# PV moved into the middle of the score bursts of a sigmoid-attention + ReGLU kernel, with wider loads, a split first load and a held weight load

## The chip, the cores and the metric

The kernel runs on one core of one Trainium2 chip. The metric is the device time of one execution in microseconds. Before the change it is 450.13 us, the median of three runs (450.03 to 451.05). The profiled execution, from which all other numbers of this part come, has a span of 453.1 us.

## What is computed

Eight batches of sigmoid attention (12 heads, 448 tokens, head size 64) feed a gated feed-forward layer. Inputs and output are float32 in DRAM; the kernel computes in float16 with float32 sums.

```python
def _attn_ref(q, k, v):                      # (8, 12, 448, 64) each
    S = q.shape[2]
    scale = 1.0 / np.sqrt(q.shape[-1])
    scores = scale * np.matmul(q, k.transpose(0, 1, 3, 2)) - np.log(S)
    attn = 1.0 / (1.0 + np.exp(-scores))
    return np.matmul(attn, v).astype(np.float32)

def _moe_ref(x, w_gate, w_val, w_out):       # x: 3584 x 768, w_gate/w_val: 768 x 1536, w_out: 1536 x 768
    gate = np.maximum(x @ w_gate, 0.0)
    val = x @ w_val
    return (gate * val @ w_out).astype(np.float32)
# x is the attention output with the heads of a token side by side
```

## The kernel before

A batch has three head groups g of four heads, and each group seven chunks c of 64 keys. One `qk_unit` makes the scores of one chunk and four heads with four 64x64 matmuls that run side by side in the array, into two PSUM banks; ScalarE then takes the sigmoid of each bank into a PT tile. `pv` sums a group's seven PT tiles times v with 28 matmuls into two banks, which VectorE scales into the xT tiles. The feed-forward part is cut into pieces that are mixed in between: `gv` (letter f in a mix) makes one slice of gate and value in two banks; `down` (letter y) makes 128 rows of output in two banks.

```python
    PTp = ctx.enter_context(tc.tile_pool(name="PTp", bufs=12))
    # (cut) PSUM: two rings of four banks, taken in turn four by four, eight banks in all
    def next_ring():
        i = turn[0] // 4 % len(rings)
        turn[0] += 1
        return rings[i]

    def rows_of(src, b, r):
        return src[b].rearrange("(g r h) (t c) d -> r t g h (c d)", r=2, h=2, c=NCH)[r]

    def load(b, g0, g1, which="kqv", c0=0):
        for nm, t16, src in zip("kqv", tiles_of(b), (k, q, v)):
            if nm in which:
                for g in range(g0, g1):
                    for r in range(2):
                        nc.gpsimd.dma_start(
                            t16[64 * r : 64 * r + 64, g, :, c0 * D :],
                            rows_of(src, b, r)[:, g, :, c0 * D :],
                        )
    # (cut) the first keys and queries come as float32 over the queues of SyncE and ScalarE:
    # k head 0, k head 1, then q chunks 0 to 2; each in two halves of 64 partitions

    def qk_unit(b, g, c):
        ps = [bank("qk_ps") for _ in range(2)]
        for r in range(2):
            for hh in range(2):
                qk(qkT_tiles[(b, g)], r, hh, c, 0, NCH, ps[hh][64 * r : 64 * r + 64, 0:S])
        PT = PTp.tile([P, 2, 512], FP16, tag="PT", name="PT")
        for hh in range(2):
            sigmoid(PT[:, hh, 0:S], ps[hh][:, 0:S])          # ScalarE
        PT_tiles[(b, g, c)] = PT

    def pv(b, g, q0, qn, pieces):
        ps = [bank("pv_ps") for _ in range(2)]
        # (cut) 28 matmuls of 64x64
        for r in range(2):
            put_xT(b, 2 * g + r, q0, qn, ps[r][:, 0:qn])     # VectorE

    def dma_transposes(b, g):
        # (cut) two VectorE copies into rel, then
        nc.sync.dma_start_transpose(qkT_of(b, g)[:], rel[:].rearrange("p c x -> p (c x)"))

    for b in range(1, B):
        cuts = (0, 4, 7, 11, 16, 21) if b <= 2 else (0, 4, 8, 12, 16, 21)
        pv_at = {0: -1, 3: 0, 4: 1} if b <= 2 else {0: -1, 2: 0, 4: 1}
        # (cut) mixes of b == 1 and b == 2
        elif b % 2:
            mix = ["fyf", "fyf", "ffff", "fyf", "fyf"]
        else:
            mix = ["fff", "fyf", "fyf", "fff", "fyf"]
        for m in range(5):
            if m in pv_at and (b, m) != (1, 0):
                if m == 0:
                    pv_finish(b - 1)          # last group of the batch before, then its gv pieces queue up
                else:
                    pv_group(b, pv_at[m])
            for g, c in order[cuts[m] : cuts[m + 1]]:
                qk_unit(b, g, c)
            if b == 1:
                if m == 0:
                    load(2, 0, 1, "kq")
                    load_o()                  # the down weights wo, float32 4.7 MB in DRAM
                    load(2, 1, 2, "kq")
                    load(2, 2, 3, "kq")
                    load(2, 0, 3, "v")
                if m == 3:
                    dma_transposes(2, 0)
            # (cut) the others of b == 2: dma_transposes(2, 1) at m 0, (2, 2) at m 1
            ffn_mix(mix[m], hooks.get(m, ()))
```

So each batch has five bursts of 64x64 matmuls (m = 0 to 4), with gv and down pieces after each.

Of the kernel before, what the change touches and what calls it, by code (L numbers as in the profile page):

```python
# [10 lines left out]
FP32 = mybir.dt.float32  # L11
# [6 lines left out]
def kernel(  # L18
# [10 lines left out]
    nc = tc.nc  # L29

    B, H, S, D = q.shape
    DM, DF = moe_w_gate.shape
    NPAIR = H // 2
    NG = H // 4
    P = 128
    NCH = S // 64
# [3 lines left out]
    QCUT = 3  # L40
# [15 lines left out]
    ysbp = ctx.enter_context(tc.tile_pool(name="ysbp", bufs=4))  # L56
# [29 lines left out]
            )  # L86
        return in_tiles[b]

    def rows_of(src, b, r):
        return src[b].rearrange("(g r h) (t c) d -> r t g h (c d)", r=2, h=2, c=NCH)[r]  # L90

    def load(b, g0, g1, which="kqv", c0=0):
        for nm, t16, src in zip("kqv", tiles_of(b), (k, q, v)):
            if nm in which:
                for g in range(g0, g1):
                    for r in range(2):
                        nc.gpsimd.dma_start(  # L97
                            t16[64 * r : 64 * r + 64, g, :, c0 * D :],
                            rows_of(src, b, r)[:, g, :, c0 * D :],
                        )  # L100


    first32 = []
    k32 = [ysbp.tile([P, DM], FP32, tag="ysb", name="ysb") for _ in range(2)]
    q32 = ysbp.tile([P, DM], FP32, tag="ysb", name="ysb")
    q32v = q32[:, 0 : 2 * QCUT * D].rearrange("p (h x) -> p h x", h=2)
    for h in range(2):
        for r, eng in ((0, nc.sync), (1, nc.scalar)):
            rs = slice(64 * r, 64 * r + 64)
            eng.dma_start(k32[h][rs, 0 : NCH * D], rows_of(k, 0, r)[:, 0, h, :])  # L110
    for r, eng in ((0, nc.sync), (1, nc.scalar)):
        rs = slice(64 * r, 64 * r + 64)
        eng.dma_start(q32v[rs], rows_of(q, 0, r)[:, 0, :, 0 : QCUT * D])
    load(0, 1, 2, "kq")
    ident = const.tile([P, P], FP16, name="ident")
    make_identity(nc, ident[:])
    load(0, 2, 3, "kq")

    gate = const.tile([P, 2], FP16, name="gate")
# [26 lines left out]
    def load_o():  # L146
        for m0, m1 in ((0, 512), (512, DM)):
            nc.gpsimd.dma_start(
                wo[:, :, m0:m1], moe_w_out[:, m0:m1].rearrange("(c p) m -> p c m", p=P)
            )  # L150

    qkT_tiles = {}
# [3 lines left out]
    def keep_warm(count):  # L156
        ps = bank("warm_ps")
        for _ in range(count):
            nc.tensor.matmul(ps[:, 0:S], zeros[:, 0:P], zeros[:], start=True, stop=True)  # L159
# [6 lines left out]
    def put_xT(b, pr, q0, qn, src):  # L166
        nc.vector.tensor_scalar(  # L167
            out=xT_of(b, pr)[:, q0 : q0 + qn],
            in0=src,
            scalar1=XSCALE,  # L170
            scalar2=None,
            op0=AOP.mult,
        )
# [10 lines left out]
    def pe_transposes(b, g, ti, c0=0, c1=NCH):  # L184
        t16 = in_tiles[b][ti]
        qkT = qkT_of(b, g)
        trt = bank16("trt")
        for c in range(c0, c1):
            for h in range(2):
                nc.tensor.transpose(  # L190
                    trt[64 * h : 64 * h + 64, c * P : (c + 1) * P],
                    t16[:, g, h, c * D : (c + 1) * D],
                    ident[:],
                )
        nc.vector.tensor_copy(  # L195
            qkT[:, ti * NCH + c0 : ti * NCH + c1, :].rearrange("p c x -> p (c x)"),
            trt[:, c0 * P : c1 * P],
        )

    def dma_transposes(b, g):  # L200
        k16, q16, _ = in_tiles[b]
        rel = relp.tile([P, TW, P], FP16, tag="rel", name="rel")
        for ti, t16 in enumerate((k16, q16)):
            nc.vector.tensor_copy(  # L204
                rel[:, ti * NCH : (ti + 1) * NCH, :].rearrange("p c (h d) -> p h c d", h=2),
                t16[:, g].rearrange("p h (c d) -> p h c d", c=NCH),
            )
        nc.sync.dma_start_transpose(
            qkT_of(b, g)[:], rel[:].rearrange("p c x -> p (c x)")
        )  # L210
# [14 lines left out]
    def pv(b, g, q0, qn, pieces):  # L225
        v16 = in_tiles[b][2]
        ps = [bank("pv_ps") for _ in range(2)]
        for c in range(NCH):
            for hh in range(2):
                for r in range(2):  # L230
                    rows = slice(64 * r, 64 * r + 64)
                    nc.tensor.matmul(  # L232
                        ps[r][64 * hh : 64 * hh + 64, 0:qn],
                        v16[rows, g, hh, c * D : (c + 1) * D],
                        pieces[c][rows, hh, :],
                        start=(c == 0),
                        stop=(c == NCH - 1),
                        tile_position=(64 * r, 64 * hh),
                        skip_group_check=True,
                    )  # L240
        for r in range(2):
            put_xT(b, 2 * g + r, q0, qn, ps[r][:, 0:qn])


    class FirstSlot:
# [28 lines left out]
# [7 lines that stand above are left out]
            sigmoid(PT[:, hh, 0:S], ps[hh][:, 0:S])  # L281
        PT_tiles[(b, g, c)] = PT

    def pv_group(b, g):
        pv(b, g, 0, S, [PT_tiles.pop((b, g, c))[:, :, 0:S] for c in range(NCH)])
# [81 lines left out]
    def ffn_mix(kinds, hooks=()):  # L367
# [8 lines left out]
    nc.scalar.activation(gate[:], zeros[:, 0:2], AF.Sigmoid, bias=sig_bias, scale=qk_scale)  # L376
    keep_warm(10)
    k16, q16, _ = in_tiles[0]
    nc.vector.tensor_copy(k16[:, 0, 0, :], k32[0][:, 0 : NCH * D])
    nc.scalar.copy(k16[:, 0, 1, :], k32[1][:, 0 : NCH * D])  # L380
    nc.vector.tensor_copy(q16[:, 0, :, 0 : QCUT * D], q32v)
    pe_transposes(0, 0, 0, 0, 4)
    pe_transposes(0, 0, 1, 0, QCUT)
    pe_transposes(0, 0, 0, 4, NCH)
    slots = [FirstSlot(g, half) for half in range(2) for g in range(NG)]
    push_first(0, range(0, 4), False)

    after = {
        (0, 0): lambda: keep_warm(2),
        (0, 1): lambda: pe_transposes(0, 1, 0),  # L390
        (0, 2): lambda: pe_transposes(0, 1, 1),
        (1, 1): lambda: pe_transposes(0, 2, 0),
# [24 lines left out]
    order = [(g, c) for g in range(NG) for c in range(NCH)]  # L417

    def pv_finish(b):
        pv_group(b, NG - 1)  # L420
        push_gv(b, 0, S, range(NFC))
        if b % 2:
            push_down(b // 2, range(7))
# [2 lines left out]
    rings.insert(0, ctx.enter_context(tc.tile_pool(name="ring1", bufs=4, space=bass.MemoryType.PSUM)))  # L426
    turn[0] = 0

    def both(b, g):
        pe_transposes(b, g, 0)  # L430
        pe_transposes(b, g, 1)

    ffn_mix("ff", [(1, lambda: both(1, 0))])
    for b in range(1, B):
        cuts = (0, 4, 7, 11, 16, 21) if b <= 2 else (0, 4, 8, 12, 16, 21)
        pv_at = {0: -1, 3: 0, 4: 1} if b <= 2 else {0: -1, 2: 0, 4: 1}
        hooks = {}
        if b == 1:
            mix = ["f" * n for n in (4, 4, 3, 4, 3)]
            hooks = {1: [(1, lambda: both(1, 1))], 2: [(1, lambda: both(1, 2))]}  # L440
        elif b == 2:
            mix = ["fff", "fff", "ffy", "fyf", "fyf"]
        elif b % 2:
            mix = ["fyf", "fyf", "ffff", "fyf", "fyf"]
        else:
            mix = ["fff", "fyf", "fyf", "fff", "fyf"]
        for m in range(5):
            if m in pv_at and (b, m) != (1, 0):
                if m == 0:
                    pv_finish(b - 1)  # L450
                else:
                    pv_group(b, pv_at[m])
            for g, c in order[cuts[m] : cuts[m + 1]]:
                qk_unit(b, g, c)
            if b == 1:
                if m == 0:
                    load(2, 0, 1, "kq")
                    load_o()
                    load(2, 1, 2, "kq")
                    load(2, 2, 3, "kq")  # L460
                    load(2, 0, 3, "v")
                if m == 3:
                    dma_transposes(2, 0)
            elif b == 2:
                if m < 2:
                    dma_transposes(2, m + 1)
                if m == 1:
                    nc.gpsimd.tensor_copy(gate[0:1, :], qkT_tiles[(2, 2)][0:1, 0, 0:2])
                    load(3, 0, 3)
            elif m == 0:  # L470
                dma_transposes(b, 2)
                if b + 1 < B:
                    load(b + 1, 0, 3)
            if m >= 3 and b >= 2 and b + 1 < B:
                dma_transposes(b + 1, m - 3)
            ffn_mix(mix[m], hooks.get(m, ()))
    pv_finish(B - 1)
    for work in (gv_queue, y_queue):
# [32 lines left out]
```

## Time and profile before

| engine | busy us | share of the span |
|---|---|---|
| TensorE matmul (PE) | 434.1 | 96% |
| ScalarE (ACT) | 211.9 | 47% |
| VectorE (DVE) | 129.6 | 29% |
| GpSimd (POOL) | 97.7 | 22% |

In the page's second part the span is cut into 40 slices of 11.3 us. A digit is a busy share in tenths; PEclk is the TensorE clock that the throttle granted, DMA the busy share of the 16 DMA engines.

```profile
PE   5999997999999999999999999999999999999995
PEclk8599998999999999999999999999999999999999
DMA  9999999999989033982449323641333101100144
```

TensorE is busy throughout, but for the first slice and the seventh, at about 70 us. Its clock is low in the second slice. The DMA engines are full for the first 11 slices. Matmul records overlap, as a record of 350 ns is followed by the next after 189 ns, so that a busy share of 96% does not say how many matmuls of full pace fit: for that the distances between starts are read.

### The profile page before, as it was taken

What the parts mean: (1) busy time and instruction counts of PE and PEld (TensorE: products, weight loads), DVE (VectorE), ACT (ScalarE), POOL (GpSimd) and SP (SyncE); (2) the same over time, 40 slices, a digit from 0 to 9 for tenths busy, and PEclk for the clock granted to TensorE, in tenths of its full rate; (3) what the DMA queues carried; (4) which work ended last, traced back from release to release, by engine and by line L of the source; (5) the groups of instructions that cost most, each with busy time, mean ns of one, the idle gap of its engine ahead of it and who ended that gap; (6) DMA issues with size and microseconds to landing.
All of it is one profiled execution on the core that took longest, in us unless ns stands there. A gap on an engine that the chain in (4) does not pass through costs nothing.

```text
span 453.1 us, 8742 instructions
## 1 busy us (share of the span) xinstructions
PE 434.1 (96%) x3660; PEld 241.8 (53%) x3660; DVE 129.6 (29%) x247; ACT 211.9 (47%) x453; POOL 97.7 (22%) x163
## 2 busy tenths in 40 slices
PE   5999997999999999999999999999999999999995
PEld 2677864455555555455455554555455545555563
DVE  1343342222331322322331232312322222222211
ACT  2685666445544445545644445444545454222110
POOL 8755613086053000630026000300000000000000
PEclk8599998999999999999999999999999999999999
DMA  9999999999989033982449323641333101100144
GB/s 162 165 198 198 165 175 159 114 135 174 141 121 194 23 76 64 133 140 51 66 73 196 62 42 77 90 63 31 68 77 77 35 1 36 35 1 0 36 104 104
DMA packets 71078, 43.75 MB, mean 97 GB/s; under 512 B 36352, under 2 KB 67456, under 8 KB 71040
## 3 DMA queue, kind: packets, MB, share of 16 engines
q0 software_dynamic: 32960, 23.28, 36.8%
q1 hardware_dynamic: 37696, 19.54, 23.6%
q8 instruction: 28, 0.46, 0.4%
q10 hardware_dynamic: 384, 0.39, 0.3%
q14 instruction: 10, 0.08, 0.1%
HBM read 47.19 MB, written 11.01 MB: 128 GB/s over the span
## 4 chain that ended last, share of the span: by engine, by line
PE 87%; DMA 5%; DVE 3%; ACT 3%; issue 1%; ACTq 0%
PE g_ps L293 24%; PE v_ps L293 23%; PE ya L331 16%; PE yb L331 8%; PE qk_ps L215 7%; PE pv_ps L232 7%; DMA qkT<-rel 3%; DVE xT L167 3%; ACT PT L176 3%; PE trt L190 2%; DMA ysb<-in_q_dram 1%; DVE qkT L195 0%; ACTq L110 0%; PE warm_ps L159 0%; ACT ysb L345 0%
## 5 line engine op out<-in xcount | busy, mean ns | idle before, releaser
L176 ACT ACTIVATE PT<-qk_ps 128x448 f16<-128x448 f32 (+3 forms) x318 | 150.8, 596 | 65.2 <-PE qk_ps L215 65.1
L293 PE MATMUL g_ps<-xT,wg 128*128 128x448 f16 (+2 forms) x648 | 128.5, 334 | 0.8 <-DVE xT L167 0.2
L293 PE MATMUL v_ps<-xT,wv 128*128 128x448 f16 (+2 forms) x648 | 127.6, 333 | 0.0
L311 DVE TENSOR_TENSOR hT<-gate_sb,v_ps 128x448 f16<-128x448 f32 (+2 forms) x108 | 60.9, 569 | 229.0 <-PE v_ps L293 118.5
L331 PEld LDWEIGHTS <-hT 128*128 128x128 f16 x672 | 65.7, 98 | 47.1
L302 ACT ACTIVATE gate_sb<-g_ps 128x448 f32<-128x448 f32 (+2 forms) x104 | 55.3, 549 | 73.1 <-PE g_ps L293 71.3
L293 PEld LDWEIGHTS <-wv 128*128 128x128 f16 x648 | 62.7, 98 | 48.3 <-issue 2.0
L293 PEld LDWEIGHTS <-wg 128*128 128x128 f16 x648 | 59.9, 98 | 48.4 <-issue 9.7
L331 PE MATMUL ya<-wo,hT 128*128 128x512 f16 x336 | 77.1, 379 | 0.0
L215 PE MATMUL qk_ps<-qkT 64*64 64x448 f16 (+2 forms) x756 | 56.2, 347 | 9.1 <-DVE xT L167 4.8
L97 POOL DMA_DIRECT2D v<-in_v_dram x48 | 29.0, 620 | 140.6 <-PE qk_ps L215 135.5
L345 ACT ACTIVATE ysb<-yb 128x256 f32<-128x256 f32 x28 | 10.7, 383 | 93.2 <-PE yb L331 93.2
L215 PEld LDWEIGHTS <-qkT 64*64 64x64 f16 x756 | 25.3, 110 | 38.2 <-issue 25.9
L331 PE MATMUL yb<-wo,hT 128*128 128x256 f16 x336 | 41.3, 273 | 0.0
L232 PE MATMUL pv_ps<-PT,v 64*64 64x448 f16 (+2 forms) x756 | 38.1, 338 | 0.1
L167 DVE TENSOR_SCALAR xT<-pv_ps 128x448 f16<-128x448 f32 (+2 forms) x54 | 28.4, 568 | 23.2 <-PE pv_ps L232 23.2
L97 POOL DMA_DIRECT2D q<-in_q_dram x48 | 28.8, 622 | 18.7 <-DMA wo<-in_moe_w_out_dram 15.8
L339 DVE TENSOR_SCALAR ysb<-ya 128x512 f32<-128x512 f32 x28 | 19.4, 692 | 46.9 <-PE ya L331 46.9
L97 POOL DMA_DIRECT2D k<-in_k_dram x46 | 27.9, 640 | 14.3 <-DMA v<-in_v_dram 7.9
L232 PEld LDWEIGHTS <-v 64*64 64x64 f16 x756 | 20.5, 111 | 15.1 <-issue 7.3
L195 DVE COPY qkT<-trt 128x896 f16<-128x896 f16 (+2 forms) x14 | 7.5, 555 | 6.5 <-PE trt L190 6.4
L204 DVE COPY rel<-k 128x896 f16<-128x896 f16 x18 | 6.9, 385 | 1.6 <-DMA k<-in_k_dram 1.6
(24 smaller groups left out, 48.0 us busy)
## 6 DMA issues: line engine op xcount, KB each, us to landing
out_dram<-ysb SPq DMA_DIRECT2D x54, 192.0 KB, 2.7
v<-in_v_dram POOLq DMA_DIRECT2D x48, 112.0 KB, 5.2
k<-in_k_dram POOLq DMA_DIRECT2D x46, 112.0 KB, 6.4
q<-in_q_dram POOLq DMA_DIRECT2D x46, 112.0 KB, 5.1
wg<-in_moe_w_gate_dram POOLq DMA_DIRECT2D x6, 384.0 KB, 9.8
wv<-in_moe_w_val_dram POOLq DMA_DIRECT2D x6, 384.0 KB, 10.0
wo<-in_moe_w_out_dram POOLq DMA_DIRECT2D x1, 1536.0 KB, 13.2
wo<-in_moe_w_out_dram POOLq DMA_DIRECT2D x1, 768.0 KB, 20.8
```

Of the source, the lines that this page charges most:

```text
L97: nc.gpsimd.dma_start(t16[64 * r : 64 * r + 64, g, :, c0 * D :], rows_of(src, b, r)[:, g, :, c0 * D :],)
L167: nc.vector.tensor_scalar(out=xT_of(b, pr)[:, q0 : q0 + qn], in0=src, scalar1=XSCALE, scalar2=None, op0=AOP.mult,)
L176: nc.scalar.activation(PT_ap, ps_ap, AF.Sigmoid, bias=sig_bias, scale=qk_scale)
L190: nc.tensor.transpose(trt[64 * h : 64 * h + 64, c * P : (c + 1) * P], t16[:, g, h, c * D : (c + 1) * D], ident[:],)
L215: nc.tensor.matmul(out_ap, qkT[rows, c, cols], qkT[rows, NCH + c0 : NCH + c1, cols], start=True, stop=True, tile_position=(64 * hh, 64 * r ...
L232: nc.tensor.matmul(ps[r][64 * hh : 64 * hh + 64, 0:qn], v16[rows, g, hh, c * D : (c + 1) * D], pieces[c][rows, hh, :], start=(c == 0), sto ...
L293: nc.tensor.matmul(ps[-1][:, 0:qn], wt[:, dc, f * P : (f + 1) * P], xT_tiles[(b, dc)][:, q0 : q0 + qn], start=(dc == 0), stop=(dc == NDC - 1),
L302: nc.scalar.activation(gate_sb[:, 0:qn], ps[0][:, 0:qn], AF.Relu)
L311: nc.vector.tensor_tensor(out=hT_tiles[(g, f)][:, o : o + qn], in0=gate_sb[:, 0:qn], in1=ps[1][:, 0:qn], op=AOP.mult,)
L331: nc.tensor.matmul(ps[:, 0 : m1 - m0], hT_tiles[(g, f)][:, t * P : (t + 1) * P], wo[:, f, m0:m1], start=(f == 0), stop=(f == NFC - 1),)
L339: nc.vector.tensor_scalar(out=ysb[:, m0:m1], in0=ps[:], scalar1=OUT_SCALE, scalar2=None, op0=AOP.mult)
L345: nc.scalar.activation(ysb[:, m0:m1], ps[:, 0 : m1 - m0], AF.Copy, scale=OUT_SCALE)
```

## The change

It has five parts. (1) In batches 2 to 7 the five bursts hold 5, 3, 5, 3 and 5 score units (before 4, 4, 4, 4, 5, in batch 2 4, 3, 4, 5, 5), and the PV of a burst comes after its second unit instead of before its first; in batch 1 the cuts stay and PV comes after the first unit. (2) A load of q, k or v takes all heads of one half of the partitions in one transfer: heads 0 to 5 lie in partitions 0 to 63, heads 6 to 11 in the others. (3) The first keys come in two pieces, chunks 0 to 3 of both heads ahead of the queries and the rest after them; the two filler matmuls behind the first unit go, and the transposes of the later keys take their place. (4) The down weights are held back: GpSimd waits for the first transposes of batch 2 before it issues them, and the keys and queries of batch 2 go ahead of them. (5) The transposes of batch 2 and the load of batch 3 come one burst or more earlier.

```diff
-    def rows_of(src, b, r):
-        return src[b].rearrange("(g r h) (t c) d -> r t g h (c d)", r=2, h=2, c=NCH)[r]
+    def rows_of(src, b, r, g0, g1, c0, c1):
+        hs = src[b, 6 * r + 2 * g0 : 6 * r + 2 * g1]
+        return hs.rearrange("h (t c) d -> t h (c d)", c=NCH)[:, :, c0 * D : c1 * D]
...
+    KCUT = 4
+    for src, c0, c1 in ((k, 0, KCUT), (q, 0, QCUT), (k, KCUT, NCH)):
...
         for r, eng in ((0, nc.sync), (1, nc.scalar)):
...
+            eng.dma_start(t32[64 * r : 64 * r + 64], rows_of(src, 0, r, 0, 1, c0, c1))
-    load(0, 1, 2, "kq")
     ident = const.tile([P, P], FP16, name="ident")
     make_identity(nc, ident[:])
+    load(0, 1, 2, "kq")
...
-            put_xT(b, 2 * g + r, q0, qn, ps[r][:, 0:qn])
+            put_xT(b, NG * r + g, q0, qn, ps[r][:, 0:qn])
...
-        (0, 0): lambda: keep_warm(2),
+        (0, 0): lambda: pe_transposes(0, 0, 0, KCUT, NCH),
...
+    def hold(b, g):
+        nc.gpsimd.tensor_copy(gate[0:1, :], qkT_tiles[(b, g)][0:1, 0, 0:2])
...
-        cuts = (0, 4, 7, 11, 16, 21) if b <= 2 else (0, 4, 8, 12, 16, 21)
-        pv_at = {0: -1, 3: 0, 4: 1} if b <= 2 else {0: -1, 2: 0, 4: 1}
+        cuts = (0, 4, 7, 11, 16, 21) if b == 1 else (0, 5, 8, 13, 16, 21)
+        pv_at = {3: 0, 4: 1} if b == 1 else {0: -1, 2: 0, 4: 1}
...
-            if m in pv_at and (b, m) != (1, 0):
-                if m == 0:
-                    pv_finish(b - 1)
-                else:
-                    pv_group(b, pv_at[m])
-            for g, c in order[cuts[m] : cuts[m + 1]]:
+            for i, (g, c) in enumerate(order[cuts[m] : cuts[m + 1]]):
+                if i == (1 if b == 1 else 2) and m in pv_at:
+                    if m == 0:
+                        pv_finish(b - 1)
+                    else:
+                        pv_group(b, pv_at[m])
                 qk_unit(b, g, c)
+            if m >= 3 and b + 1 < B:
+                dma_transposes(b + 1, m - 3)
+            if m == 0 and b > 1:
+                dma_transposes(b, 2)
             if b == 1:
                 if m == 0:
                     load(2, 0, 1, "kq")
-                    load_o()
                     load(2, 1, 2, "kq")
                     load(2, 2, 3, "kq")
+                if m == 3:
+                    hold(2, 0)
+                    load_o()
                     load(2, 0, 3, "v")
...
+            elif m == 0 and b + 1 < B:
+                if b == 2:
+                    hold(2, 2)
+                load(b + 1, 0, 3)
```

The purpose: VectorE is to empty the two PV banks while TensorE still has score units to do, no burst is to reach the banks that were filled just before it, the first score unit is to start on less data, and the transposes of batch 2 are not to share the DMA engines with the down weights.

More of the change, by code (lines that the diff above doesn't have):

```diff
@@ L94, in load @@
             if nm in which:
[L95 to L100, printed above, removed]
+                for r in range(2):
+                    nc.gpsimd.dma_start(
+                        t16[64 * r : 64 * r + 64, g0:g1, :, c0 * D :].rearrange(
+                            "t g h x -> t (g h) x"
+                        ),
+                        rows_of(src, b, r, g0, g1, c0, NCH),
+                    )
+    KCUT = 4
     first32 = []
[L104 to L107, printed above, removed]
+    for src, c0, c1 in ((k, 0, KCUT), (q, 0, QCUT), (k, KCUT, NCH)):
+        ysb = ysbp.tile([P, DM], FP32, tag="ysb", name="ysb")
+        t32 = ysb[:, 0 : 2 * (c1 - c0) * D].rearrange("p (h x) -> p h x", h=2)
         for r, eng in ((0, nc.sync), (1, nc.scalar)):
[L109 to L113, printed above, removed]
-    load(0, 1, 2, "kq")
+            eng.dma_start(t32[64 * r : 64 * r + 64], rows_of(src, 0, r, 0, 1, c0, c1))
+        first32.append(t32)
     ident = const.tile([P, P], FP16, name="ident")
     make_identity(nc, ident[:])
+    load(0, 1, 2, "kq")
     load(0, 2, 3, "kq")
@@ L378 @@
     k16, q16, _ = in_tiles[0]
[L379 to L382, printed above, removed]
+    nc.vector.tensor_copy(k16[:, 0, :, 0 : KCUT * D], first32[0])
+    nc.scalar.copy(q16[:, 0, :, 0 : QCUT * D], first32[1])
+    pe_transposes(0, 0, 0, 0, KCUT)
     pe_transposes(0, 0, 1, 0, QCUT)
-    pe_transposes(0, 0, 0, 4, NCH)
+    nc.vector.tensor_copy(k16[:, 0, :, KCUT * D :], first32[2])
     slots = [FirstSlot(g, half) for half in range(2) for g in range(NG)]
@@ L457 @@
                     load(2, 0, 1, "kq")
-                    load_o()
                     load(2, 1, 2, "kq")
                     load(2, 2, 3, "kq")
+                if m == 3:
+                    hold(2, 0)
+                    load_o()
                     load(2, 0, 3, "v")
[L462 to L475, printed above, removed]
+            elif m == 0 and b + 1 < B:
+                if b == 2:
+                    hold(2, 2)
+                load(b + 1, 0, 3)
             ffn_mix(mix[m], hooks.get(m, ()))
```

## The prediction

> **What bounds the kernel now.** I read the page first: TensorE is busy 96% of the span, and the chain that ended last is 87% TensorE, so only what lets TensorE start its next matmul earlier counts. The list of waits by engine, cut to TensorE, names what it waits for (total us, times, longest):
>
> ```profile
> PE qk_ps L215 <- DVE xT L167: 4.8, 29, 0.2
> PE qk_ps L215 <- DMA qkT<-rel: 2.4, 1, 2.4
> PE trt L190 <- ACT k L380: 2.4, 1, 2.4
> ```
>
> The first is a wait that recurs in each burst with PV, the second happens once, the third once at the start. Idle time understates the first: a matmul record lasts 350 ns but its successor normally starts after 189 ns, so a late start shows only in part as a gap. I therefore read starts in the timeline, around one burst without PV and one with PV and five units (start, duration, engine):
>
> ```profile
> 211.76 1.23 PE L215 MATMUL qk_ps<-qkT 64*64 64x448 f16 x16
> 211.94 0.62 DVE L311 TENSOR_TENSOR hT<-gate_sb,v_ps 128x448 f16<-128x448 f32 x1 [2.96 <-PE v_ps L293]
> 212.18 3.60 ACT L176 ACTIVATE PT<-qk_ps 128x448 f16<-128x448 f32 x8 [0.91 <-PE qk_ps L215]
> 212.61 0.11 PEld L215 LDWEIGHTS <-qkT 64*64 64x64 f16 x2 [0.34 <-issue]
> 212.92 1.31 PE L293 MATMUL g_ps<-xT,wg 128*128 128x448 f16 x6
> ...
> 219.84 1.52 PE L232 MATMUL pv_ps<-PT,v 64*64 64x448 f16 x28
> 221.18 0.74 PE L215 MATMUL qk_ps<-qkT 64*64 64x448 f16 x12
> 221.40 1.16 DVE L167 TENSOR_SCALAR xT<-pv_ps 128x448 f16<-128x448 f32 x2 [0.77 <-PE pv_ps L232]
> 222.08 0.35 PE L215 MATMUL qk_ps<-qkT 64*64 64x448 f16 x1 [0.15 <-DVE xT L167]
> 222.61 0.57 PE L215 MATMUL qk_ps<-qkT 64*64 64x448 f16 x7 [0.18 <-DVE xT L167]
> 223.11 1.31 PE L293 MATMUL g_ps<-xT,wg 128*128 128x448 f16 x6
> ```
>
> The reader is to see two PSUM waits. With PV: PV takes two banks, three units take six, and the fourth unit needs the PV banks again. VectorE empties them by 222.02 and 222.56; the two matmuls start 0.05 us after each. From PV's start to the gate matmul it is 3.27 us. Without PV: four units take eight banks, and the last is the one of the value matmul just before, which VectorE empties from 211.94 to 212.56; the fourth unit goes on at 212.61, and the burst lasts 1.165 us. A burst of three units (85.13 us, batch 2) lasts 0.694 us.
>
> Two one-time losses stand in the chain and the timeline (start, duration):
>
> ```profile
> 2.08 6.46 DMA ysb<-in_q_dram
> 59.71 15.45 DMA qkT<-rel
> 76.60 2.18 PE g_ps L293 x6
> 78.78 1.88 PE v_ps L293 x6
> 80.66 1.14 PE g_ps L293 x6
> ```
>
> The first query transfer, issued behind all the first keys, takes 6.46 us; the first score matmul starts at 9.97. The transposes of batch 2, group 0, take 15.45 us, while the median from issue to landing of these 18 transfers is 5.3; then six gate matmuls take 2.18 us instead of 1.14.
>
> [...] the distances in bank turns above fit eight. [...] while the transposes' packets run, from about 63 to 75 us, GpSimd's own queue falls from 205 KB to about 130 KB per us. [...] here the granted clock is at half from 76.8 to 80.2 us, after TensorE's stall, and from 8.5 to 22.1 us.
>
> **PV third, bursts of 5 and 3 (batches 2 to 7).** I count from a burst's first matmul. Units start at 0 and 0.19; PV runs from 0.40 for 1.35; unit three starts at 1.75, four at 1.94, five at 2.13. Banks: two units take 1 to 4, PV 5 and 6, unit three 7 and 8, unit four 1 and 2, unit five 3 and 4. So nobody in the burst waits for PV's banks. Bank 8 was the value's, free at 0.80 (212.56 less 211.76), needed at 1.75. Banks 1 to 4 come back from the sigmoids: the first starts at 0.42 (212.18 less 211.76), eight take 3.60, which is 0.58 for one and 0.43 for each further, so they end at 1.00, 1.43, 1.86 and 2.29. Unit four, at 1.94, is free; unit five waits for the fourth sigmoid, 2.29 + 0.05 = 2.34. From the second matmul of a last unit to the gate matmul it is 0.31 (212.92 less 212.61), so the burst lasts 2.65 us. VectorE starts on PV's banks 1.56 after PV's start (221.40 less 219.84), at 1.96, and frees the first at 2.58 + 0.05 = 2.63: the gate's bank is just in time, the value's (3.2) is needed at 3.8. A burst of three takes six banks, does not touch the last value's, and takes 0.694.
>
> Before, a batch of five bursts takes, by the same starts, 3.08 + 1.165 + 2.77 + 1.165 + 3.27 = 11.45 us (batch 4; batches 3 to 7 lie between 11.40 and 11.46). After: 3 x 2.65 + 2 x 0.694 = 9.34. Saved: 2.1 us in each of six batches (batch 2 without its stall has 11.4 too), together **12.5 us**. The number of changes between 64x64 and 128x128 matmuls stays five a batch, so that cost is unchanged. In batch 1 the fifth unit meets PV's banks: PV starts at 0.19, the second bank is free at 0.19 + 1.56 + 1.16 + 0.05 = 2.97, burst 3.28, as before: nothing. PT has 12 buffers; at most 11 units are alive when a PV frees seven, so no sigmoid waits.
>
> **Down weights held.** Before, the stall costs 76.535 - 71.256 = 5.28 us for a burst that takes 3.08 elsewhere, and the slow clock makes the next gate and value 3.96 instead of 2.28: 2.2 + 1.7 = **3.9 us** that should go, as the transposes of group 0 now meet only the end of the key and query loads. But group 1's transposes are issued one burst later, at about 64, together with the held weights; the third unit of the second burst of batch 2, which needs them, comes at about 78. At 130 KB per us the weights (2.36 MB as float16) run to about 80, and the transposes next to them took 15.45 before: 64 + 15 = 79. I set a new stall of 0 to 3 us, **1.0** in the mean.
>
> **First keys in two pieces.** Before the first score matmul, the queues of SyncE and ScalarE bring 655 KB (keys 459, queries 196); after, 262 + 196 = 458 KB, and GpSimd's loads start behind the identity. I estimate keys at 4.0, queries at 5.2; cast, transposes and copy as in the trace about 1.8 more, so the first score matmul at about 7.0 instead of 9.97. The fillers that go took 0.86 (10.44 to 11.30), the six key transposes that come take 0.5 there: 3.3 us in all. A limit follows soon: the DMA engines are full to 56 us, and the bytes ahead stay the same. The v of batch 1 lands at 52.7 and is used at 56.3: 3.6 us of slack (the weights of slices 2 and 3: 25.7 against 29.6). I take **3.3 us**.
>
> **Loads of all heads.** A batch takes 6 issues of some 0.6 us instead of 18, so 7 us less on GpSimd. GpSimd is idle two thirds of the time and no wait of TensorE on a load stands in the list: 0.
>
> Sum: 450.1 - 12.5 - 3.9 + 1.0 - 3.3 = 431.4; I say 431.5.
>
> **Rivals.** (a) ScalarE takes over: ten sigmoids run to 4.9 us after a burst's start, and the gate's ReLU queues behind them. For it: unit five already waits on sigmoid four. Against: ScalarE is busy 47% and the gate's bank comes round only eight banks later. If each long burst lost 0.5 us, 18 bursts would give 9 back: 440. (b) The stall moves from group 0 to group 1 of batch 2, or to the v of batch 2, which now stands behind the weights and is needed at about 85. For it: 79 against 78 above. With a slow clock behind it the whole 3.9 comes back: 434 to 436. (c) The start is hidden: the early gain ends in waiting for weights or v, since DMA is the bound to 52.7. Gain 0 to 1: 434. The other way, a clock that stays full from 8.5 on could bring more, but no more than the 3.6 of slack.
>
> **Range and chances.** The 12.5 rests on repeated starts to a few hundredths; (a) is its only threat. The one-time terms can be off by 3 each way. That gives 427 to 438. A gain over 2% needs less than 441.1, which takes (a), (b) and (c) together: 0.93 faster, 0.06 same, 0.01 slower.
>
> **What would show it.** In the changed profile: no wait of score matmuls on xT in batches 2 to 7, a short one on PT instead; long bursts of 2.65 and short ones of 0.69 us; the first score matmul near 7; no 15 us transposes of group 0 in the chain. Wrong would be: long bursts over 2.9, gate matmuls waiting on xT, or a wait on the transposes of group 1 or on v of batch 2 over 2 us with a half clock behind it.

## The result, and the profile after

The changed kernel takes 440.14 us (median of four, 440.0 to 440.84); the kernel before, on the same chip, 450.08. The ratio is 0.978, with a 95% interval of 0.976 to 0.980. Predicted were 431.5 us and a range of 427 to 438, so the sign was right and the size about twice too large: 9.9 us were gained where 18.6 were forecast.

The profiled execution after has a span of 438.4 us. TensorE's waits in it, in the view of waits shown for before (total us, times, longest):

```profile
PE qk_ps L214 <- DMA qkT<-rel: 2.9, 1, 2.9
PE trt L189 <- ACT q L379: 1.4, 1, 1.4
PE qk_ps L214 <- DVE xT L166: 0.3, 2, 0.2
```

The 29 waits on xT have become two, both in batch 1. A single wait on the DMA transposes is still there, 2.9 us instead of 2.4, and one at the start is still there, now for the queries' cast.

The timeline after, a short burst and a long one (start, duration, engine):

```profile
204.75 0.76 PE L214 MATMUL qk_ps<-qkT 64*64 64x448 f16 x12
...
205.45 1.31 PE L292 MATMUL g_ps<-xT,wg 128*128 128x448 f16 x6
...
212.36 0.57 PE L214 MATMUL qk_ps<-qkT 64*64 64x448 f16 x8
212.76 1.49 PE L231 MATMUL pv_ps<-PT,v 64*64 64x448 f16 x28
212.79 3.16 ACT L175 ACTIVATE PT<-qk_ps 128x448 f16<-128x448 f32 x7 [0.91 <-PE qk_ps L214]
214.09 0.98 PE L214 MATMUL qk_ps<-qkT 64*64 64x448 f16 x12
214.30 1.16 DVE L166 TENSOR_SCALAR xT<-pv_ps 128x448 f16<-128x448 f32 x2 [1.14 <-PE pv_ps L231]
214.69 0.11 PEld L214 LDWEIGHTS <-qkT 64*64 64x64 f16 x2 [0.30 <-issue]
...
215.00 0.74 PE L292 MATMUL g_ps<-xT,wg 128*128 128x448 f16 x3
```

The short burst lasts 0.70 us (204.75 to 205.45) and the long one 2.64 (212.36 to 215.00), where the prediction had 0.694 and 2.65. The fifth unit's second half goes on at 214.69, 2.33 after the burst's start, on the fourth sigmoid's bank, as worked out (2.34). The change from 128x128 to 64x64 matmuls takes what it took before: 0.28 us from the last value matmul to the first score matmul in both traces (211.48 to 211.76 before, 212.08 to 212.36 after), where value matmuls follow each other at 0.19. VectorE empties PV's banks from 214.30 to 215.46, and nobody in the burst waits for it.

The new loss is in the chain that ended last (first three lines: start, duration) and in the timeline at 78 us:

```profile
66.04 15.51 DMA qkT<-rel
81.97 2.36 PE g_ps L292 x6
84.33 1.69 PE v_ps L292 x6
...
78.15 0.57 PE L214 MATMUL qk_ps<-qkT 64*64 64x448 f16 x8
81.59 0.38 PE L214 MATMUL qk_ps<-qkT 64*64 64x448 f16 x4 [2.87 <-DMA qkT<-rel]
```

The transposes of batch 2, group 1, issued at 66.04, take 15.51 us. The two units of group 0 run at 78.15, then TensorE stands still to 81.59, and the next gate and value run at half pace. From the burst's start to the gate it is 3.76 us instead of 0.69, gate and value take 3.95 instead of 2.28: 4.7 us in all. It looks like the old loss, one group later: group 0's transposes keep the place that they had before, group 1's come one burst earlier than before and now run beside the held weights, which are issued from 63.61 on. Whether the weights are the reason is tried below.

### The profile page after: what moved, and what is told of

It is laid out like the page before. It is cut to its first block, busy times and chain, and to the rows that moved or that the text cites. A ratio compares the mean times of both kernels' runs of the same rounds, so it can differ in the third digit from the quotient of the medians.

```text
span 438.4 us, 8643 instructions
## 1 busy us (share of the span) xinstructions
PE 425.8 (97%) x3658; PEld 239.3 (55%) x3658; DVE 130.3 (30%) x247; ACT 212.5 (48%) x453; POOL 57.8 (13%) x92
## 4 chain that ended last, share of the span: by engine, by line
PE 91%; DMA 5%; ACT 1%; DVE 1%; issue 1%; SPq 0%; ACTq 0%
PE g_ps L292 25%; PE v_ps L292 24%; PE ya L330 17%; PE qk_ps L214 9%; PE yb L330 8%; PE pv_ps L231 7%; DMA qkT<-rel 4%; PE trt L189 2%; ACT PT L175 1%; DMA ysb<-in_q_dram 1%; DVE xT L166 1%; DVE qkT L194 0%; SPq L111 0%; ACT q L379 0%; ACT ysb L344 0%
## 5 line engine op out<-in xcount | busy, mean ns | idle before, releaser
L214 PE MATMUL qk_ps<-qkT 64*64 64x448 f16 (+2 forms) x756 | 53.0, 349 | 5.2 <-DMA qkT<-rel 2.9
L214 PEld LDWEIGHTS <-qkT 64*64 64x64 f16 x756 | 21.5, 110 | 31.7 <-issue 21.1
L97 POOL DMA_DIRECT2D v<-in_v_dram x16 | 11.2, 708 | 172.0 <-PE qk_ps L214 168.9
L231 PEld LDWEIGHTS <-v 64*64 64x64 f16 x756 | 22.4, 112 | 11.2 <-issue 0.9
L97 POOL DMA_DIRECT2D q<-in_q_dram x28 | 17.6, 643 | 3.3 <-DMA k<-in_k_dram 1.8
L97 POOL DMA_DIRECT2D k<-in_k_dram x26 | 16.5, 642 | 7.9 <-DMA wv<-in_moe_w_val_dram 4.0
L203 DVE COPY rel<-q 128x896 f16<-128x896 f16 x18 | 7.8, 436 | 0.0
```

Source lines behind the costliest of these rows:

```text
L97: nc.gpsimd.dma_start(t16[64 * r : 64 * r + 64, g0:g1, :, c0 * D :].rearrange("t g h x -> t (g h) x"), rows_of(src, b, r, g0, g1, c0, NCH),)
L214: nc.tensor.matmul(out_ap, qkT[rows, c, cols], qkT[rows, NCH + c0 : NCH + c1, cols], start=True, stop=True, tile_position=(64 * hh, 64 * r ...
L231: nc.tensor.matmul(ps[r][64 * hh : 64 * hh + 64, 0:qn], v16[rows, g, hh, c * D : (c + 1) * D], pieces[c][rows, hh, :], start=(c == 0), sto ...
```

## The experiments

Each ratio is taken from medians beside runs of the kernel before on the same chip (449.4 to 449.8 us there), with its 95% interval in brackets. Variants that are set against each other ran mostly on different chips. Executions of one kernel differ by some us (the kernel before from 448.0 to 454.3 on these chips), so most intervals reach about 0.6% to each side, and differences of 1 us between two variants are not resolved.

### The kernel before, profiled again

The first profile of before is of an execution of 454.94 us, 4.8 above the timed median. The kernel is unchanged.

> The kernel before, unchanged, profiled once more. Theory A: the profiled execution of before (454.94 us) held a loss of some 4.8 us that its timed executions (450.08) do not have, and the likeliest is the wait for the transposes of batch 2, group 0, with the half clock behind it (3.9 us by the first profile); then this execution takes about 450 us, and its trace shows a short wait or none at about 72 us. Theory B: every profiled execution of before is slower than the timed ones; then about 455 us with the same wait of 2.4 us. Theory C: the 4.8 us lie in the start, in a clock that stays at half for longer; then the first weights' matmul at another time than 24.3 us.

It took 450.06 us, with a span of 448.2. Its wait and the six gate matmuls behind it:

```profile
PE qk_ps L215 <- DMA qkT<-rel: 1.8, 1, 1.8
...
72.04 1.40 PE L215 MATMUL qk_ps<-qkT 64*64 64x448 f16 x16 [1.75 <-DMA qkT<-rel]
73.37 1.31 PE L293 MATMUL g_ps<-xT,wg 128*128 128x448 f16 x6
```

The wait is there, but a little shorter, and the gate behind it runs at full pace (1.31 us against 2.24 in the first profile). From PV's start to the gate this burst takes 4.60 us (68.77 to 73.37) instead of 3.08, so the wait costs 1.5 us, not 3.9. The first gate matmul comes at 21.86 instead of 24.34. Those two places hold the difference of the spans: 2.5 us at the start, 0.7 of wait and 1.7 of half clock are 4.9. Theory A was right in part, for the wait is short but not gone. Theory C was too: of the 2.5 us at the start 1.4 are there before any score matmul (the first is at 8.60 here, at 9.97 in the first profile, as keys and queries came later), and only the other 1.1 arise while TensorE runs at half pace, to 17 us here and to 22 in the first profile.

### The removed wait alone

```diff
-                if m == 3:
-                    dma_transposes(2, 0)
...
-            hooks = {1: [(1, lambda: both(1, 1))], 2: [(1, lambda: both(1, 2))]}
+            hooks = {..., 4: [(1, lambda: both(2, 0))]}     # on TensorE, kernel before otherwise
```

> The kernel before with the keys and queries of batch 2, group 0, transposed by TensorE in batch 1, so that the wait that the change was to remove is gone and nothing else. If the wait costs timed executions what the first profile showed (2.2 us and 1.7 of half clock): 449.7 - 3.9 + 0.9 = 446.7 us. If it costs them what the second profile of before showed (1.5 us, no half clock): 449.7 - 1.5 + 0.9 = 449.1 us.

450.01 us against 449.39, ratio 1.001 (0.9995 to 1.003); no wait on transposes is left in its trace, but three more short ones on xT (32 instead of 29). With 0.9 us of added transposes the wait was worth 0.4 us to timed executions (-0.4 to 1.1, from the ratio), even less than the second profile's 1.5. So, by that interval, at least 2.8 of the prediction's 3.9 us were not in the time that it started from.

### The new wait, taken away in two ways

First, group 1 of batch 2 is transposed on TensorE in the changed kernel:

```diff
-            if m >= 3 and b + 1 < B:
+            if m >= 3 and b + 1 < B and (b, m) != (1, 4):
                 dma_transposes(b + 1, m - 3)
...
+            hooks = {..., 4: [(1, lambda: both(2, 1))]}
```

> The changed kernel with the keys and queries of batch 2, group 1, transposed by TensorE in batch 1 instead of by DMA under the down weights. If the wait of 3.0 us at 78 us and the half clock behind it (together 4.7 us) come from these transposes meeting the weights: 0.9 us of transposes come and 4.7 go, 440.1 - 3.8 = 436.3 us. If another transfer takes the place of the wait (v of batch 2, group 2): 438 to 440 us.

436.02 us, ratio 0.967 (0.961 to 0.974). No wait on the transposes is left. Then the transposes stay with DMA and the weights get out of their way:

```diff
                 if m == 3:
-                    hold(2, 0)
-                    load_o()
                     load(2, 0, 3, "v")
+                if m == 4:
+                    hold(2, 1)
+                    load_o()
```

> The changed kernel with the down weights held until the transposes of batch 2, group 1 (not group 0) have landed, and the v of batch 2 ahead of them. If the wait at 78 us comes from group 1's transposes sharing the DMA engines with the weights, they land some 5 us after their issue, near 70 us, the wait of 3.0 us and the half clock (1.7 us) go: 440.1 - 4.7 = 435.4 us. If the weights then come too late for the first down piece at about 93 us, or group 2's transposes for theirs, a wait comes back: 438 us or more.

435.72 us, ratio 0.967 (0.960 to 0.975). How group 1's transposes fare, from the view of transfers between 60 and 90 us of the changed kernel, and between 65 and 68 us of this one, in which no other transfer runs then (transfer, queue, count, median us to landing):

```profile
qkT<-rel SPq DMA_TRANSPOSE x2, 15.9
```

```profile
qkT<-rel SPq DMA_TRANSPOSE x1, 4.0
```

Beside the weights 15.9 us (the median of groups 1 and 2), alone 4.0. Against 439.93 us, a repetition of the changed kernel (below), the two ways give back 4.2 and 4.8 us (436.02 holds 0.9 us of transposes). That the new wait comes from the transposes meeting the held weights is shown, and its cost agrees with the 4.7 us read from the trace.

### The bursts alone, and their two halves

In the kernel before, batches 3 to 7 alone get the new bursts:

```diff
-        cuts = (0, 4, 7, 11, 16, 21) if b <= 2 else (0, 4, 8, 12, 16, 21)
+        cuts = (0, 4, 7, 11, 16, 21) if b <= 2 else (0, 5, 8, 13, 16, 21)
...
+            for i, (g, c) in enumerate(order[cuts[m] : cuts[m + 1]]):
+                if i == (0 if b <= 2 else 2) and m in pv_at and (b, m) != (1, 0):
+                    (PV as before)
                 qk_unit(b, g, c)
```

> The kernel before with the new bursts alone, in batches 3 to 7: 5, 3, 5, 3, 5 units, PV after the second. The prediction's working gives 2.1 us a batch: 10.4 us less, 439.7 us, ratio 0.977. If the bursts are worth less in time than in the starts of the trace, over 443 us.

439.68 us against 449.83, ratio 0.976 (0.970 to 0.983): 10.1 us, predicted 10.4. Alone, this part does as much as the whole change, as far as the intervals tell.

Which half carries it? From the kernel with group 1 on TensorE (436.02 us), PV goes back before the first unit with sizes 5 and 3 kept, or the sizes go back with PV kept third:

```diff
-                if i == (1 if b == 1 else 2) and m in pv_at:
+                if i == (1 if b == 1 else 0) and m in pv_at:      # PV first
```

```diff
-        cuts = ... if b == 1 else (0, 5, 8, 13, 16, 21)
+        cuts = ... if b == 1 else (0, 4, 8, 12, 16, 21)           # sizes 4, 4, 4, 4, 5
```

> The kernel with group 1 transposed on TensorE (436.0 us), bursts of 5 and 3 kept, but PV before the first unit in batches 2 to 7. By the prediction's bank counting the fifth and fourth units then meet PV's banks again: long bursts of 3.2 to 3.3 us instead of 2.64, short ones of 0.69: 3 x 0.61 x 6 = 11.0 us more, 447.0 us. If the sizes 5 and 3 carry the gain and the place of PV does not matter: 436 to 438 us.

447.37 us, ratio 0.993 (0.990 to 0.995): 11.35 us more. Long bursts last 3.2 to 3.3 us again (3.22 from 213.98), short ones 0.70, and TensorE's waits again hold what before showed:

```profile
PE qk_ps L214 <- DVE xT L166: 4.9, 30, 0.2
```

> The kernel with group 1 transposed on TensorE (436.0 us), PV kept after the second unit, but bursts of 4, 4, 4, 4, 5 units in batches 2 to 7. By bank counting a burst of four with PV waits for nothing (2.23 us), a burst of four without PV waits for the last value's bank (1.165): 2.23 x 2 + 1.165 x 2 + 2.64 = 9.43 against 9.31 a batch: 0.7 us more, 436.7 us. If the sizes matter as much as the place: 440 us or more.

436.95 us, ratio 0.970 (0.963 to 0.978): 0.9 us more than 436.02. The intervals overlap, so the time alone does not show a difference; the starts do. A burst of four with PV, in its timeline:

```profile
219.69 0.57 PE L214 MATMUL qk_ps<-qkT 64*64 64x448 f16 x8
220.09 1.49 PE L231 MATMUL pv_ps<-PT,v 64*64 64x448 f16 x28
221.42 0.55 PE L214 MATMUL qk_ps<-qkT 64*64 64x448 f16 x8
221.90 1.33 PE L292 MATMUL g_ps<-xT,wg 128*128 128x448 f16 x6
```

It lasts 2.21 us (2.23 expected) and waits for nothing; bursts of four without PV take 1.16 again (200.43 to 201.59). So the place of PV is worth about 11 us, the sizes 5 and 3 about 0.4 by the starts (9.38 against 9.31 in each of six batches), which the time does not resolve.

### The start

The changed kernel with the first loads of before (keys whole, then queries, fillers kept):

```diff
-    for src, c0, c1 in ((k, 0, KCUT), (q, 0, QCUT), (k, KCUT, NCH)):
+    (k head 0, k head 1, then q chunks 0 to 2, as before)
...
-        (0, 0): lambda: pe_transposes(0, 0, 0, KCUT, NCH),
+        (0, 0): lambda: keep_warm(2),
```

> The changed kernel with the first loads of the kernel before (keys whole, then queries; fillers kept). By the traces the split gave 2.0 us: 442.1 us. If DMA is the bound of the first 50 us and the gain is given back there: 440 us. By the prediction's 3.3 us: 443.4.

439.46 us, ratio 0.975 (0.969 to 0.980). The changed kernel took 440.14, and 439.93 in a repetition: the split is worth nothing that is resolved here. A reason may lie in TensorE's pace: by the changed kernel's profile the first score matmul is at 8.00 us, 0.6 sooner than in the second profile of before, yet the first gate matmul is at 22.34, later than the 21.86 there.

```profile
8.60 0.53 PE L215 MATMUL qk_ps<-qkT 64*64 64x192 f16 x8
```

```profile
8.00 0.53 PE L214 MATMUL qk_ps<-qkT 64*64 64x192 f16 x8 [0.46 <-DVE qkT L194]
```

That was tried with fillers, matmuls on zeros that keep TensorE busy, on the version with group 1 on TensorE:

```diff
     pe_transposes(0, 0, 0, 0, KCUT)
+    keep_warm(5)
     pe_transposes(0, 0, 1, 0, QCUT)
...
+        (0, 3): lambda: keep_warm(2),
+        (1, 3): lambda: keep_warm(2),
```

> The kernel with group 1 transposed on TensorE (436.0 us), with nine filler matmuls where TensorE waits in the first 16 us: five while the first queries are cast, two each behind the last unit of the first two slots. Theory: the early start is lost because TensorE runs at half clock to 17 to 22 us[...]; fillers bring the full clock[...] earlier: 434 to 435 us, and less spread between executions. Rival: DMA or ScalarE bound the first 20 us: 436 us, or 437 with the fillers' own time.

434.43 us (433.77 to 435.49), ratio 0.965 (0.958 to 0.972), 1.6 less than without (435.48 to 437.36). The same 14 key transposes, in the timeline of the changed kernel and of this one:

```profile
9.44 0.96 PE L189 MATMUL trt<-ident,k 128*64 128x128 f16 x14
```

```profile
9.34 0.58 PE L189 MATMUL trt<-ident,k 128*64 128x128 f16 x14
```

In all twelve profiles without these fillers the 14 transposes take 0.77 to 0.96 us, in all five with them 0.58. Here the pace becomes full at about 3.9 us, before the first of the added fillers at 5.2, and stays full. The split itself, with the pace kept at full in both, tried by giving this version the first loads of before (five fillers then stand ahead of the key transposes, and the two behind the first unit stay):

> The version with fillers and group 1 on TensorE (434.4 us), with the first loads of the kernel before. With the clock at full from the start in both, what is left is the split itself: the first score matmul comes 0.3 to 0.7 us later and two fillers of 0.4 us stay. If that reaches the end: 435.2 us. If it is hidden: 434.4 us. The prediction's 3.3 us would make 437.7.

435.15 us, ratio 0.967 (0.961 to 0.972): 0.7 more than 434.43, near the expected 0.8, but the ranges of the two overlap (434.28 to 436.35). So with the pace at full in both the split is worth about 0.7 us, not resolved, and not 3.3.

### The wide loads

```diff
-                for r in range(2):
-                    (one transfer, all groups of half r)
+                for g in range(g0, g1):
+                    for r in range(2):
+                        (one transfer for group g, half r)
```

Beside a repetition of the changed kernel:

> The changed kernel, unchanged, as the measure for the others of this set: 440.1 us, with the wait of about 3 us for group 1's transposes at 78 us.

> The changed kernel with one transfer for each head group and half, as before (18 a batch instead of 6). The prediction gives the wide loads nothing: the same time as the changed kernel, 440.1 us within 0.7. If the many small transfers hold up GpSimd's queue at the start, 441 us or more; if wide loads delay the first group's v, 439.

439.93 us for the changed kernel, ratio 0.978 (0.972 to 0.983), with the wait of 2.9 us as before. With small transfers 441.82 (438.34 to 443.25), ratio 0.980 (0.973 to 0.987). Repeated with fillers and group 1 on TensorE:

> The version with fillers and group 1 on TensorE (434.4 us), with one transfer for each head group and half. The loads alone, without the wait at 78 us and with a full clock at the start: if the wide loads are worth nothing, 434.4 us within 0.7. If the small transfers themselves cost (the other comparison gave 441.8 against 439.9, with a spread of 5 us): 436 us.

435.55 us (434.39 to 436.85), ratio 0.970 (0.966 to 0.973), against 434.43. They point to 1.9 and 1.1 us in favour of the wide loads, and neither resolves it. Whether they are worth anything is left open.

### A version faster than both

Held weights and fillers together, without transposes on TensorE:

> The changed kernel with the weights held for group 1's transposes, v ahead of them (435.7 us alone), and the nine fillers in the first 16 us. No transposes on TensorE, so 0.9 us less than the version with fillers and group 1 on TensorE (434.4): 433.5 us. If holding the weights costs something elsewhere: 434.5 or more.

435.78 us, ratio 0.968 (0.961 to 0.975): the expectation failed. Its chain in the window from 55 us on begins:

```profile
54.35 13.52 DMA qkT<-rel
...
67.91 0.96 PE qk_ps L214 x6
```

TensorE reaches batch 2 at 65.0, 3.6 us sooner than in the changed kernel (68.6), and waits to 67.9, now for group 0: its transposes meet the v that was moved ahead. So v goes behind them:

```diff
                 if m == 3:
+                    hold(2, 0)
                     load(2, 0, 3, "v")
                 if m == 4:
                     hold(2, 1)
                     load_o()
```

> The version with fillers and held weights, with the v of batch 2 now behind group 0's transposes as in the changed kernel, the weights behind group 1's. In the version before it (435.8 us) v ran beside group 0's transposes, which landed at 67.9, and TensorE, 2 us earlier than elsewhere, waited 2.9 us for them. If that was v's doing: no wait at 65 us, 435.8 - 2.9 and less the half clock: 432 to 433.5 us. If TensorE is now simply too early for group 0: 435 or more.

432.35 us (431.81 to 433.40), ratio 0.9625 (0.960 to 0.965), no wait on transposes: 7.6 us below the repetition of the changed kernel. In the view of its waits TensorE now waits for the v of batch 0 in the first 20 us, at 14.2:

```profile
PE pv_ps L231 <- DMA v<-in_v_dram: 0.8, 1, 0.8
```

## Why the prediction was right in sign and wrong in size

**PV third, bursts of 5 and 3: right.** Predicted 12.5 us. The starts give 11.43 - 9.31 = 2.1 a batch, 12.7 for six, and the part alone took 10.1 us of time for five batches. The bank counting held to 0.01 us for both bursts, and putting PV first again cost 11.35 where 11.0 was expected. One small term was missed: in batch 1 the burst of PV and five takes 2.96 us (54.29 to 57.25), not 3.28, so 0.3 in each of two bursts.

**Down weights held: wrong, and the larger error.** Two terms of this step failed. The term "2.2 + 1.7 = 3.9 us that should go" took the loss from a profile of 454.94 us and subtracted it from a time of 450.13 us that contained little of it; the page's time and the timed median stood side by side and their difference of 4.8 us was not asked about. Timed executions had 0.4 us of it (-0.4 to 1.1). And the term "I set a new stall of 0 to 3 us, 1.0 in the mean" was mis-sized: the two times set against each other were near (79 against 78 predicted, 81.5 against 78.5 in the trace), but the wait alone adds 3.07 us to its burst, and the half clock behind it, another 1.67, was left out: 4.7 us where 1.0 was set. The mechanism, named there and in rival (b), is the one shown. Together the two terms took 7.2 us off (3.5 + 3.7).

**First keys in two pieces: wrong.** "3.3 us" rested on queries at 5.2 and a first score matmul at 7.0. GpSimd's first load was issued at 1.44, only 0.2 us later than before, not behind a long make_identity; the queries came at 6.4 and the first score matmul at 8.0. That is 2.0 sooner than in the first profile, but only 0.6 sooner than in the second (8.6), and it is about 0.7, unresolved, in time. This step left out TensorE's pace, which behind the first score matmul was low in every profile without the added fillers (0.77 to 0.96 us for 14 transposes instead of 0.58); why the queries took 4.8 us to land is open.

**Loads of all heads: 0 predicted**, not refuted and not shown. (GpSimd is idle 78% of the time by the page, not two thirds, which does not weaken the argument.)

The sum with measured terms, on the chip of the repetition: 449.7 - 12.7 - 0.6 - 0.4 + 4.7 - 0 = 440.7, against 439.9 measured; the 0.8 left is in reach of the start and the loads, which were not resolved. Rival (a), ScalarE, did not come: 2.64 us a long burst. Rival (c) was near in its number (a gain of 0 to 1 at the start) and not by its reason: the changed kernel's waits hold none for weights or v, and fillers alone still gained 1.6. Waits for such data show only in two versions with fillers: 0.8 us for v in the fastest one, 0.7 for value weights in the one with small transfers.

## What to carry to other kernels

Where an engine waits for buffers to be emptied, count the bank turns in program order and put work between the producer and its reuse; here that is worth 11 us, and the arithmetic holds to a few hundredths. Before a one-time loss in a profile is subtracted, compare the profiled execution's time with the timed median: a loss that the timed executions do not have cannot be gained. And when a transfer is moved away from a waiting consumer, list every other transfer that then runs beside it: here the wait moved to the next one in line, from group 0's transposes (2.4 us in the first profile) to group 1's (2.9), and with v moved ahead back to group 0's (2.9).

## What was not expected of the hardware

From 18 us on the traces hold ten stalls of TensorE of over 1.5 us, as the view of waits counts them. Three are not followed by a lower clock: 1.8 us in the second profile of before (granted clock 1.00 from 64 to 88 us), and 2.07 each in the bursts alone (0.998 in the mean of the run) and in the version with held weights (1.00 from 20 to 30 us). The seven from 2.4 to 3.3 us are each followed by a stretch of half clock, in the first profile of before from 76.8 to 80.2 us and in the changed kernel from 81.9 to 85.3, 3.4 us in both. Whether the length of a stall alone decides it, ten stalls do not tell.

The granted clock in the windows view is not always what the matmuls ran at: for the changed kernel it says 1.00 from 10 to 20 us, where 14 transposes take 0.96 us instead of 0.58. Here the pace of like instructions was the safer sign.

In the version with held weights and in the one with small transfers (its profiled execution is the longest of its four) TensorE stood for 2.1 and 2.9 us near 20 us within the same PV, both times after its 15th matmul (the other 13 start at 20.65 and at 21.72), with nothing that the profile names as the cause.

In the version with held weights, from 18 to 21 us, the DMA engines are busy over 90% in every slice of the view of transfers, and one packet of 0.02 MB runs on the queue that the profile names "instruction". Whether the stall has to do with either was not tried.
